# A DFT and a gated FFN on one Trainium2 core: raw weights kept in buffers of `h`, part of the weight fold and of stage 2 moved between FFN steps, and the mirror value matmul behind the next chunk's gate matmuls

## The chip, the cores and the metric

The kernel runs on one core of one Trainium2 chip. The metric is the device time of one execution in microseconds (us); lower is better. Every time quoted is a median of several executions on the chip, with the lowest and highest in brackets. A profile, taken by the hardware profiler, shows one execution of each kernel; its span is about 1.7 us shorter than the time.

The engines are called as the profile calls them: PE is the matmul side of TensorE and PEld its weight loads, DVE is VectorE, ACT is ScalarE, POOL is GpSimd, SP is SyncE (here it only issues DMAs).

## The reference, cut to what matters

```python
# x: (8, 3008, 256) f32; w_gate, w_val: (256, 1536) f32; w_out: (1536, 256) f32
X = np.fft.fft(np.fft.fft(x, axis=1), axis=2).real      # per batch
t = X.reshape(8 * 3008, 256)
out = (np.maximum(t @ w_gate, 0) * (t @ w_val)) @ w_out  # f32
```

The kernel factors the long DFT as 3008 = 94 x 32. The 256-point DFT is not done on the data at all: it is multiplied into the two weight matrices once ("fold of the weights"), which gives three sets of folded weights, `wc` and `ws` for cosine and sine and `wm` = -2·`ws` (with an exception in row 0). The outputs come in pairs of frequencies k and -k. For one chunk of 128 hidden units, "plus" computes the pre-activations of k as `wc·p + ws·q`; "minus" (the mirror) adds `wm·q` into the same PSUM accumulator, which turns it into `wc·p - ws·q`, the pre-activations of -k. `G` and `V` are these accumulators for the gate and the value weights, the tile `pq` holds p and q, `gs` is the rectified G, and `h` is the product of `gs` and V (the gate product).

## The kernel before

There are 8 batches of 3 blocks of 12 chunks: 288 FFN steps. The data of the next batches go through stage 1, a shuffle through DRAM, a rotation and stage 2 in small pieces between the FFN steps. Only batch 0 has to do all that first, together with the tables and the fold of the weights. That is "the start" below.

```python
def fold(b, eng, lo, hi):            # symmetric parts of x; four passes over n rows, on DVE or POOL
    xl, xh, xc, eo = xt[b]
    n = hi - lo
    x1, c1, e1 = xl[:, lo:hi, :], xc[:, lo - 1:hi - 1, :], eo[:, lo:hi, :]
    rev = free(xh[0:NA], (NB // 2 - lo) * D, [-D, n], [1, D])
    eng.tensor_tensor(c1, x1, rev, op=ALU.subtract)
    eng.tensor_tensor(x1, x1, rev, op=ALU.add)
    ...                              # two more passes that write eo, and a small copy

def rotate(b):                       # needs all of the shuffle's loads
    t4 = t4t[b]
    ps = psd.tile([128, 512], F32, tag="d", name="psr")
    nc.tensor.matmul(ps[:, 0:NKA], lhsT=rot[:], rhs=t4[:, :, H], start=True, stop=True)
    nc.vector.tensor_copy(t4[:, :, H], ps[:, 0:NKA])
...
    # ---- the start, in program order (tables left out) ----
    fold(0, nc.vector, 2, 8); fold(0, nc.vector, 8, 12)      # on separate lines in the kernel
    fold(0, nc.gpsimd, 12, 16)
    fold_ends(0, nc.vector)
    fold(0, nc.vector, 1, 2)
    for k, c in enumerate((1, 2, 3, 4, 5, 6, 7, 0)):
        stage1(0, c, "dve" if k in (5, 7) else "act")
    for k in (2, 4, 6, 0):
        shuffle_out(0, k, k + 2)                             # to DRAM
    load_x(1, nc.scalar)                                     # next batch, 1.6 MB and a gather of 1.6 MB
    nc.gpsimd.dma_start(out=wo[:], in_=view(w_out, ...))     # 768 KB
    for blk in range(NBLK):
        shuffle_in(0, 4 * blk, 4 * blk + 4)                  # back from DRAM
    fold_all(1)
    for n in range(DF // 512):                               # fold of the weights, fp32
        for i in range(2):
            for cs in range(2):
                ps = psw.tile([128, 512], F32, tag="w", name="psw")
                for c in range(2):
                    nc.tensor.matmul(ps[:], lhsT=cd[:, c, cs, :], rhs=wst[i][:, c, n * 512:(n + 1) * 512],
                                     start=(c == 0), stop=(c == 1))
                ...                                          # copies to wc, or to ws and wm
    rotate(0)
    for blk in range(NBLK):
        stage2(0, blk, 0, "act"); stage2(0, blk, 1, "dve")
...
def plus(b, blk, f):
    ...                                                      # h, G (psg, 2 buffers), V (psv, 2 buffers)
    for i, acc in enumerate((G, V)):
        nc.tensor.matmul(acc[:], lhsT=wc[i][:, fs], rhs=pq[:, 0, :], start=True, stop=False)
        nc.tensor.matmul(acc[:], lhsT=ws[i][:, fs], rhs=pq[:, 1, :], start=False, stop=True)
    gs = gp.tile([128, 512], F32, tag="gs", name="gs")
    nc.scalar.activation(gs[:], G[:], ACTF.Relu)
    nc.vector.tensor_tensor(h[:, 0, :], gs[:], V[:], op=ALU.mult)      # the gate product

def minus(b, blk, f):
    ...
    for i, acc in enumerate((G, V)):
        nc.tensor.matmul(acc[:], lhsT=wm[i][:, fs], rhs=pq[:, 1, :], start=False, stop=True,
                         skip_group_check=True)
    gs = gp.tile([128, 512], F32, tag="gs", name="gs")
    nc.scalar.activation(gs[:], G[:], ACTF.Relu)
    nc.vector.tensor_tensor(free(h[:], ...), gs[:]..., V[:]..., op=ALU.mult)
...
for b in range(B):
    t0 = b * NBLK * NF
    tl, t1, tr, t2, d2 = (17, 16, 28, 29, 1) if b == 0 else (10, 4, 19, 20, 2)
    ...    # at step t0+tl: load x of b+2; from t0+t1: stage 1 of b+1; t0+tr: rotate; from t0+t2: stage 2
for t in range(n + NF):
    if 0 < t <= n:
        minus(*steps[t - 1])
    if t < n:
        plus(*steps[t])
    for fn in extra.get(t, ()):
        fn()
    if t >= NF:
        out_piece(b, blk, f)           # 8 output matmuls of the step 12 earlier
```

The order of the matmuls in one step is therefore: mirror G, mirror V (of the chunk before), plus G (two), plus V (two), then eight output matmuls. Mirror V overwrites the accumulator that the gate product of the step before reads. The output matmuls lag by 12 steps, so the first 12 steps, called the ramp, have none.

## Time and profile before

The time is 752.1 us (751.9 to 754.2, four executions). Five readings matter.

| reading | value |
|---|---|
| rotation of batch 0 starts | 67.67 us |
| first FFN matmul | 70.87 us |
| first output matmul (ramp 27.55 us long) | 98.42 us |
| median step after that | 2.217 us |
| start of the last output matmul to the end of the span | 5.6 us |

The chain that ended last, from the profile's page, first by engine and then by line:

```profile
PE 82%; DVE 6%; ACT 4%; POOL 3%; issue 3%; DMA 1%; ACTq 0%; POOLq 0%; DVEq 0%
PE po L380 30%; PE V L357 10%; PE G L347 7%; PE G L346 7%; PE V L347 7%; PE V L346 7%; PE G L357 7%; DVE h L350 4%; PE psw L313 3%; ACT gs L360 2%; ACT gs L349 1%; DVE h L362 1%; DMA t_969<-Td 1%; DMA Td<-t_719 1%; DVE q L37 0%
```

Mirror V (L357 V) holds 10% of the chain where each other FFN matmul of the same size holds 7%, and DVE's gate product (L350) holds 4%. Those are the first signs that mirror V is held up by DVE. The table by stages says almost nothing of it. Its columns are the stretch in us, then for PE, PEld, DVE, ACT and POOL the busy time with the number of instructions, then the granted TensorE clock, the DMA share and GB/s:

```profile
60.00:70.00 10.00, 8.69 (x34) 3.90 (x34) 2.98 (x6) 4.03 (x7) 8.67 (x2) 1.00 0.81 154
80.00:90.00 10.00, 7.34 (x29) 2.62 (x28) 6.24 (x10) 5.38 (x9) 9.11 (x7) 1.00 0.14 30
200.00:400.00 200.00, 199.53 (x1331) 126.65 (x1330) 136.96 (x209) 118.74 (x206) 65.93 (x25) 1.00 0.37 94
```

From 200 to 400 us PE is shown busy for 199.53 of 200 us. That looks like a limit with nothing left to gain. It isn't, because the ends of matmuls are modelled: a matmul is drawn 0.38 us long and the next may start 0.215 us after it. The page "Trainium Kernel Development and Optimization" of the Trainium skill (section "Performance Expectations") warns that matmul busy time is a bad measure of how near a kernel is to its limit, since matmuls are pipelined. This trace agrees: PE is drawn busy for 199.53 of 200 us, and only the spacing from start to start shows the hole. Here is one steady step in the timeline (start, duration, engine, line, operation; in brackets, idle time and what ended it):

```profile
277.24 0.69 DVE L350 TENSOR_TENSOR h<-gs,V 128x512 bf16<-128x512 f32 x1
...
277.72 0.38 PE L357 MATMUL G<-pq,wm_91 128*128 128x512 bf16 x1
...
277.99 0.38 PE L357 MATMUL V<-pq,wm_92 128*128 128x512 bf16 x1
...
278.20 0.38 PE L346 MATMUL G<-pq,wc_87 128*128 128x512 bf16 x1
```

The gate product ends at 277.93, and mirror V starts just behind it, at 277.99: 0.27 us after mirror G, where every other pair of these matmuls is 0.215 us apart (277.99 to 278.20). No idle time is drawn at mirror V, because mirror G is still drawn as running. Summed over all steps after 98 us, the spacing from mirror G to mirror V exceeds 215 ns by 14.7 us in total.

In the ramp the same dependence is not hidden in 50 ns but stands alone:

```profile
71.52 0.38 PE L347 MATMUL V<-pq,ws_90 128*128 128x512 bf16 x1
...
71.55 0.60 ACT L349 ACTIVATE gs<-G 128x512 f32<-128x512 f32 x1 [0.23 <-PE G L347]
72.20 0.38 PE L357 MATMUL G<-pq,wm_91 128*128 128x512 bf16 x1 [0.30 <-ACT gs L349]
...
72.23 0.69 DVE L350 TENSOR_TENSOR h<-gs,V 128x512 bf16<-128x512 f32 x1 [0.47 <-ACT gs L349]
...
72.98 0.38 PE L357 MATMUL V<-pq,wm_92 128*128 128x512 bf16 x1 [0.40 <-DVE h L350]
```

A ramp step is a loop of plus G, ACT 0.60, DVE 0.69, mirror V, and takes 2.22 us although its six matmuls take 1.29 us (6 x 0.215).

The third place is the start, again in the timeline:

```profile
20.75 0.30 POOL L35 TENSOR_SCALAR q<-t_204 128x128 f32<-128x128 f32 x1
20.76 1.89 DVE L88 TENSOR_TENSOR xc<-xl,xh 94x1536 f32<-94x1536 f32 x1 [4.67 <-DMA xh<-in_x_dram,ix]
21.14 1.67 POOL L36 TENSOR_SCALAR q<-q 128x128 f32<-128x128 f32 x1
22.69 1.75 DVE L89 TENSOR_TENSOR xl<-xl,xh 94x1536 f32<-94x1536 f32 x1
...
42.06 0.59 PE L117 MATMUL ps_277<-eo,w_82 94*96 94x256 bf16 x2 [8.48 <-POOL eo L92]
...
67.67 0.18 PE L146 MATMUL psr<-t_304,rot 128*128 128x12 bf16 x1 [0.39 <-DMA t_304<-Td]
```

The fold of x ends on POOL at 42.06 us. POOL's 128x128 table operation at 21.14 takes 1.67 us; its neighbour of the same size, started 0.01 us before DVE's fold operation, took 0.30 us. It ends 0.16 us after the DVE operation beside it. The rotation waits for the last load of the shuffle. PE is busy until shortly before it with the fold of the weights, 24 fp32 matmuls of about 0.86 us, which this wait just hides.

### The profile page before, as it was taken

The page shows a single profiled execution, that of the slowest core. Times are in us where ns is not written, and L with a number is a line of the kernel's source. Part 1 is how long each engine was busy: PE and PEld are TensorE (multiplying, and loading weights), DVE is VectorE, ACT ScalarE, POOL GpSimd, SP SyncE. Part 2 cuts the span into 40 slices and gives each one's busy share as a digit, 9 for nine tenths or more (in the row PEclk, how much of TensorE's full clock was granted, in tenths as well). Part 3 has the DMA queues.
Part 4 walks back from the last instruction along what each step waited for, and adds up shares of the span by engine and source line. Part 5 has one row for each costly group of instructions (what it writes and reads, how often), then busy time and mean ns, then how long its engine had stood idle before and what let it go on. Part 6 is the DMA issues. An engine that isn't in the chain of part 4 may idle for free.

```text
span 750.4 us, 12199 instructions
## 1 busy us (share of the span) xinstructions
PE 692.4 (92%) x4432; PEld 430.6 (57%) x4432; DVE 481.0 (64%) x747; ACT 408.3 (54%) x701; POOL 221.6 (30%) x116
## 2 busy tenths in 40 slices
PE   0178799999999999999999999999999999999997
PEld 0033256566666666666666666666666666666565
DVE  6613666666666766766666767666667667666672
ACT  2114556556565656556565655556565655555551
POOL 2837739102920086004900094005800000000000
PEclk9999999999999999999999999999999999999999
DMA  9466253616342534116241454135221141211213
GB/s 195 165 164 113 62 112 93 157 29 151 104 111 57 115 112 113 56 41 172 71 135 33 116 139 111 29 82 143 59 55 29 32 136 28 53 33 28 55 29 82
DMA packets 26971, 67.61 MB, mean 90 GB/s; under 512 B 3856, under 2 KB 17680, under 8 KB 24720
## 3 DMA queue, kind: packets, MB, share of 16 engines
q1 hardware_dynamic: 24340, 51.84, 26.6%
q0 software_dynamic: 2448, 13.37, 8.2%
q10 hardware_dynamic: 124, 1.64, 0.9%
q8 instruction: 34, 0.56, 0.3%
q14 instruction: 25, 0.20, 0.1%
HBM read 36.68 MB, written 30.93 MB: 90 GB/s over the span
## 4 chain that ended last, share of the span: by engine, by line
PE 82%; DVE 6%; ACT 4%; POOL 3%; issue 3%; DMA 1%; ACTq 0%; POOLq 0%; DVEq 0%
PE po L380 30%; PE V L357 10%; PE G L347 7%; PE G L346 7%; PE V L347 7%; PE V L346 7%; PE G L357 7%; DVE h L350 4%; PE psw L313 3%; ACT gs L360 2%; ACT gs L349 1%; DVE h L362 1%; DMA t_969<-Td 1%; DMA Td<-t_719 1%; DVE q L37 0%
## 5 line engine op out<-in xcount | busy, mean ns | idle before, releaser
L362 DVE TENSOR_TENSOR h<-gs,V 128x512 bf16<-128x512 f32 x288 | 198.1, 688 | 203.4 <-ACT gs L360 148.6
L380 PE MATMUL po<-wo,h 128*128 128x256 bf16 x2304 | 296.8, 272 | 0.0
L360 ACT ACTIVATE gs<-G 128x512 f32<-128x512 f32 x288 | 172.2, 598 | 214.1 <-PE G L357 214.1
L380 PEld LDWEIGHTS <-h 128*128 128x128 bf16 x2304 | 222.7, 98 | 64.1 <-issue 2.0
L350 DVE TENSOR_TENSOR h<-gs,V 128x512 bf16<-128x512 f32 x288 | 197.8, 687 | 11.3 <-ACT gs L349 9.9
L349 ACT ACTIVATE gs<-G 128x512 f32<-128x512 f32 x288 | 172.3, 598 | 30.9 <-PE G L347 14.7
L88 POOL TENSOR_TENSOR xc<-xl,xh 94x3840 f32<-94x3840 f32 (+1 forms) x8 | 60.6, 7574 | 302.2 <-DMA xl<-in_x_dram 268.8
L357 PE MATMUL V<-pq,wm_92 128*128 128x512 bf16 x288 | 108.6, 377 | 6.3 <-DVE h L350 4.2
L357 PE MATMUL G<-pq,wm_91 128*128 128x512 bf16 x288 | 109.1, 379 | 3.1 <-ACT gs L349 3.1
L347 PE MATMUL V<-pq,ws_90 128*128 128x512 bf16 x288 | 109.2, 379 | 0.0
L346 PE MATMUL V<-pq,wc_88 128*128 128x512 bf16 x288 | 109.0, 378 | 0.0
L347 PE MATMUL G<-pq,ws_89 128*128 128x512 bf16 x288 | 108.9, 378 | 0.0
L346 PE MATMUL G<-pq,wc_87 128*128 128x512 bf16 x288 | 108.8, 378 | 0.0
L89 POOL TENSOR_TENSOR xl<-xl,xh 94x3840 f32<-94x3840 f32 (+1 forms) x8 | 60.6, 7578 | 0.6
L346 PEld LDWEIGHTS <-wc_87 128*128 128x128 bf16 x288 | 27.7, 96 | 54.5 <-issue 43.2
L347 PEld LDWEIGHTS <-ws_90 128*128 128x128 bf16 x288 | 28.0, 97 | 34.2
L386 ACT COPY os<-po 128x512 f32<-128x512 f32 x48 | 28.1, 586 | 35.6 <-PE po L380 35.6
L346 PEld LDWEIGHTS <-wc_88 128*128 128x128 bf16 x288 | 27.8, 97 | 34.3
L347 PEld LDWEIGHTS <-ws_89 128*128 128x128 bf16 x288 | 27.7, 96 | 34.2
L117 PEld LDWEIGHTS <-w_82 94*96 94x96 bf16 x120 | 15.7, 131 | 50.5 <-issue 28.1
L384 DVE COPY os<-po 128x512 f32<-128x512 f32 x48 | 33.0, 688 | 6.9 <-PE po L380 6.9
L357 PEld LDWEIGHTS <-wm_92 128*128 128x128 bf16 x288 | 28.2, 98 | 9.6 <-issue 6.5
(345 smaller groups left out, 346.8 us busy)
## 6 DMA issues: line engine op xcount, KB each, us to landing
out_dram<-os SPq DMA_DIRECT2D x176, 128.0 KB, 2.1
xl<-in_x_dram SPq DMA_DIRECT2D x7, 1360.0 KB, 9.8
xl<-in_x_dram SPq DMA_DIRECT2D x7, 238.0 KB
wst_103<-in_moe_w_gate_dram SPq DMA_DIRECT2D x2, 768.0 KB, 20.4
wst_106<-in_moe_w_val_dram SPq DMA_DIRECT2D x2, 768.0 KB, 23.7
out_dram<-os SPq DMA_DIRECT2D x16, 96.0 KB, 4.5
xl<-in_x_dram ACTq DMA_DIRECT2D x1, 1360.0 KB
Td<-t_256 SPq DMA_DIRECT2D x4, 192.0 KB, 9.2
```

The costliest lines, as they stand in the source:

```text
L88: eng.tensor_tensor(c1, x1, rev, op=ALU.subtract)
L89: eng.tensor_tensor(x1, x1, rev, op=ALU.add)
L346: nc.tensor.matmul(acc[:], lhsT=wc[i][:, fs], rhs=pq[:, 0, :], start=True, stop=False)
L347: nc.tensor.matmul(acc[:], lhsT=ws[i][:, fs], rhs=pq[:, 1, :], start=False, stop=True)
L349: nc.scalar.activation(gs[:], G[:], ACTF.Relu)
L350: nc.vector.tensor_tensor(h[:, 0, :], gs[:], V[:], op=ALU.mult)
L357: nc.tensor.matmul(acc[:], lhsT=wm[i][:, fs], rhs=pq[:, 1, :], start=False, stop=True, skip_group_check=True)
L360: nc.scalar.activation(gs[:], G[:], ACTF.Relu)
L362: nc.vector.tensor_tensor(free(h[:], 512 + NB - 1, [NB, 16], [-1, NB]), gs[:].rearrange("p (a k) -> p a k", k=NB), V[:].rearrange("p (a k) ...
L380: nc.tensor.matmul(po[:, s % 2, :], lhsT=ht[b, blk, ff][:, sg, g * 128:(g + 1) * 128], rhs=wo[:, ff, :], start=(ff == 0), stop=(ff == NF - 1))
L384: nc.vector.tensor_copy(os_[:, s - 1:s + 1, :], po[:])
L386: nc.scalar.copy(os_[:, s - 1:s + 1, :], po[:])
```

## The change

The intent is to start the FFN steps earlier and to take the hole out of each step. The change has four parts.

1. The raw weights and the DFT table `cd` are now held in tiles of the pool of `h` (which isn't needed before the FFN steps), so that the fold of the weights may run late. It is cut in three: a third between stage-1 parts, a third before the rotation, a third in FFN steps 0 to 3.
2. Stage 2 of blocks 1 and 2 of batch 0 moves to FFN steps 5 to 8, and rotation and stage 2 of batch 1 move one step later.
3. In each step, mirror V moves behind plus G: mirror G, plus G (two), mirror V, plus V (two).
4. At the start, tables of `m2` and `rot` move from POOL to DVE, the table of `cd` moves just before the fold of x, POOL folds six rows instead of four, and stage-1 parts alternate with shuffle stores.

The diff, cut to its core:

```diff
+    hp = ctx.enter_context(tc.tile_pool(name="hp", bufs=2 * NF + 1, space=SB))
+    pso = ctx.enter_context(tc.tile_pool(name="pso", bufs=2, space=PS))
...
+                wst[i, n, c] = hp.tile([128, 512], F32, tag="h", name="wst")
+    cd = [hp.tile([128, 2, H], F32, tag="h", name="cd") for c in range(2)]
...
+    def fold_w(n, i, cs):
+        ps = pso.tile([128, 512], F32, tag="o", name="psw")
+        for c in range(2):
+            nc.tensor.matmul(ps[:], lhsT=cd[c][:, cs, :], rhs=wst[i, n, c][:], start=(c == 0), stop=(c == 1))
+        ...                                     # copies as before
...
-            sin_of(nc, pl, sp, sv[:], t2[:], NB, [128, 4, NB])
+            sin_of(nc, nc.vector, sp, sv[:], t2[:], NB, [128, 4, NB])
...                                             # and the other table operations beside it
-        fold(0, nc.vector, 2, 8)
-        fold(0, nc.vector, 8, 12)
-        fold(0, nc.gpsimd, 12, 16)
+        fold(0, nc.vector, 2, 6)
+        fold(0, nc.gpsimd, 10, 14)
+        fold(0, nc.vector, 6, 10)
+        fold(0, nc.gpsimd, 14, 16)
         fold_ends(0, nc.vector)
         fold(0, nc.vector, 1, 2)
-        for k, c in enumerate((1, 2, 3, 4, 5, 6, 7, 0)):
-            stage1(0, c, "dve" if k in (5, 7) else "act")
-        for k in (2, 4, 6, 0):
-            shuffle_out(0, k, k + 2)
+        for k, (c0, c1) in enumerate(((1, 3), (3, 5), (5, 7), (7, 8), (0, 1))):
+            for c in range(c0, c1):
+                stage1(0, c, "act")
+            shuffle_out(0, c0, c1)
+            if k < 2:
+                for cs in range(2):
+                    fold_w(0, k, cs)
         load_x(1, nc.scalar)
-        nc.gpsimd.dma_start(out=wo[:], in_=view(w_out, ...))
         for blk in range(NBLK):
             shuffle_in(0, 4 * blk, 4 * blk + 4)
+        nc.gpsimd.dma_start(out=wo[:], in_=view(w_out, ...))
         fold_all(1)
-        ...                                     # the whole fold of the weights
+        for i in range(2):
+            for cs in range(2):
+                fold_w(1, i, cs)
     rotate(0)
-    for blk in range(NBLK):
-        stage2(0, blk, 0, "act")
-        stage2(0, blk, 1, "dve")
+    stage2(0, 0, 0, "act")
+    stage2(0, 0, 1, "dve")
...                                             # plus and minus are cut in their G and V halves (i = 0, 1)
+    for k in range(4):
+        at(k, fold_w, 2, k // 2, k % 2)
+        at(5 + k, stage2, 0, 1 + k // 2, k % 2, "dve")
...
-        tl, t1, tr, t2, d2 = (17, 16, 28, 29, 1) if b == 0 else (10, 4, 19, 20, 2)
+        tl, t1, tr, t2, d2 = (17, 16, 29, 30, 1) if b == 0 else (10, 4, 19, 20, 2)
...
-        if 0 < t <= n:
-            minus(*steps[t - 1])
-        if t < n:
-            plus(*steps[t])
+        for i in range(2):
+            if 0 < t <= n:
+                minus(*steps[t - 1], i)
+            if t < n:
+                plus(*steps[t], i)
```

More of the change, by code (lines that the diff above doesn't have):

```diff
@@ L178 @@
     wo = const.tile([128, NF, D], BF16, tag="wo")
-    with tc.tile_pool(name="st", bufs=1, space=SB) as st, \
-         tc.tile_pool(name="sp", bufs=2, space=SB) as sp, \
-         tc.tile_pool(name="psw", bufs=4, space=PS) as psw:
-        wst = []
+    wst = {}
+    for n in range(DF // 512):
         for i, w in enumerate((w_gate, w_val)):
-            t = st.tile([128, 2, DF], F32, tag=f"wst{i}", name=f"wst{i}")
             for c in range(2):
-                nc.sync.dma_start(out=t[:, c, :], in_=w[c * 128:(c + 1) * 128, :])
-            wst.append(t)
+                wst[i, n, c] = hp.tile([128, 512], F32, tag="h", name="wst")
+    cd = [hp.tile([128, 2, H], F32, tag="h", name="cd") for c in range(2)]
+    for n in range(DF // 512):
+        for i, w in enumerate((w_gate, w_val)):
+            for c in range(2):
+                nc.sync.dma_start(out=wst[i, n, c][:], in_=w[c * 128:(c + 1) * 128, n * 512:(n + 1) * 512])
+    def fold_w(n, i, cs):
+        ps = pso.tile([128, 512], F32, tag="o", name="psw")
+        for c in range(2):
+            nc.tensor.matmul(ps[:], lhsT=cd[c][:, cs, :], rhs=wst[i, n, c][:], start=(c == 0), stop=(c == 1))
+        sl_ = slice(n * 512, (n + 1) * 512)
+        if cs == 0:
+            nc.scalar.copy(wc[i][:, sl_], ps[:])
+        else:
+            nc.vector.tensor_copy(ws[i][:, sl_], ps[:])
+            nc.scalar.activation(wm[i][:, sl_], ps[:], ACTF.Copy, scale=s2[:])
+    with tc.tile_pool(name="sp", bufs=2, space=SB) as sp:
         si = sp.tile([NA, J], F32, tag="si")
@@ L212 @@
         nc.vector.memset(w1[:, 0, :], 0.0)
-        cd = st.tile([128, 2, 2, H], F32, tag="cd")
-        for c in range(2):
-            mi = sp.tile([128, 1], F32, tag="mi")
-            nc.gpsimd.iota(mi[:], pattern=[[0, 1]], base=c * 128, channel_multiplier=1,
-                           allow_small_or_imprecise_dtypes=True)
-            dd = sp.tile([128, 2, H], F32, tag="dd")
-            nc.gpsimd.iota(dd[:], pattern=[[0, 2], [1, H]], base=0, channel_multiplier=0,
-                           allow_small_or_imprecise_dtypes=True)
-            nc.vector.memset(dd[:, 1, 0:1], float(H))
-            nc.vector.tensor_scalar(dd[:], dd[:], scalar1=mi[:], scalar2=None, op0=ALU.mult)
-            nc.vector.tensor_scalar(dd[:, 0, :], dd[:, 0, :], scalar1=float(D // 4), scalar2=None, op0=ALU.add)
-            nc.vector.tensor_scalar(dd[:, 1, 0:1], dd[:, 1, 0:1], scalar1=float(D // 4), scalar2=None, op0=ALU.add)
-            sin_of(nc, nc.vector, sp, cd[:, c, :, :], dd[:], D, [128, 2, H])
         pl = nc.gpsimd
@@ L266 @@
                        allow_small_or_imprecise_dtypes=True)
-        pl.tensor_scalar(ui[:], ui[:], scalar1=up[:], scalar2=None, op0=ALU.is_equal)
+        nc.vector.tensor_scalar(ui[:], ui[:], scalar1=up[:], scalar2=None, op0=ALU.is_equal)
         for cs in range(2):
             t2 = sp.tile([128, 4, NB], F32, tag="m2t")
-            pl.tensor_scalar(t2[:], kbi[:], scalar1=mul[:], scalar2=offs[cs][:],
+            nc.vector.tensor_scalar(t2[:], kbi[:], scalar1=mul[:], scalar2=offs[cs][:],
                                     op0=ALU.mult, op1=ALU.add)
             sv = sp.tile([128, 4, NB], F32, tag="m2s")
-            sin_of(nc, pl, sp, sv[:], t2[:], NB, [128, 4, NB])
-            pl.tensor_tensor(m2[:, cs, :].rearrange("p (u k) -> p u k", u=4), sv[:], ui[:], op=ALU.mult)
+            sin_of(nc, nc.vector, sp, sv[:], t2[:], NB, [128, 4, NB])
+            nc.vector.tensor_tensor(m2[:, cs, :].rearrange("p (u k) -> p u k", u=4), sv[:], ui[:], op=ALU.mult)
         di = sp.tile([128, 4, 2, 16], F32, tag="di")
@@ L281 @@
         pl.memset(ro[:], 0.0)
-        pl.tensor_scalar(ro[:, :, 0, 1:16], di[:, :, 0, 1:16], scalar1=16.0, scalar2=-1.0,
+        nc.vector.tensor_scalar(ro[:, :, 0, 1:16], di[:, :, 0, 1:16], scalar1=16.0, scalar2=-1.0,
                                 op0=ALU.is_equal, op1=ALU.mult)
-        pl.tensor_scalar(ro[:, :, 1, 1:16], di[:, :, 1, 1:16], scalar1=-16.0, scalar2=None, op0=ALU.is_equal)
-        pl.tensor_scalar(ro[:, :, :, 0], di[:, :, :, 0], scalar1=0.0, scalar2=None, op0=ALU.is_equal)
-        pl.tensor_copy(rot[:], ro[:].rearrange("p u s j -> p (u s j)"))
+        nc.vector.tensor_scalar(ro[:, :, 1, 1:16], di[:, :, 1, 1:16], scalar1=-16.0, scalar2=None, op0=ALU.is_equal)
+        nc.vector.tensor_scalar(ro[:, :, :, 0], di[:, :, :, 0], scalar1=0.0, scalar2=None, op0=ALU.is_equal)
+        nc.vector.tensor_copy(rot[:], ro[:].rearrange("p u s j -> p (u s j)"))
         pf = sp.tile([128, 1], F32, tag="pf")
@@ L291 @@
         pl.tensor_scalar(s2[:], pf[:], scalar1=1.0, scalar2=-2.0, op0=ALU.min, op1=ALU.mult)
-        fold(0, nc.vector, 2, 8)
-        fold(0, nc.vector, 8, 12)
-        fold(0, nc.gpsimd, 12, 16)
+        for c in range(2):
+            mi = sp.tile([128, 1], F32, tag="mi")
+            nc.gpsimd.iota(mi[:], pattern=[[0, 1]], base=c * 128, channel_multiplier=1,
+                           allow_small_or_imprecise_dtypes=True)
+            dd = sp.tile([128, 2, H], F32, tag="dd")
+            nc.gpsimd.iota(dd[:], pattern=[[0, 2], [1, H]], base=0, channel_multiplier=0,
+                           allow_small_or_imprecise_dtypes=True)
+            nc.vector.memset(dd[:, 1, 0:1], float(H))
+            nc.vector.tensor_scalar(dd[:], dd[:], scalar1=mi[:], scalar2=None, op0=ALU.mult)
+            nc.vector.tensor_scalar(dd[:, 0, :], dd[:, 0, :], scalar1=float(D // 4), scalar2=None, op0=ALU.add)
+            nc.vector.tensor_scalar(dd[:, 1, 0:1], dd[:, 1, 0:1], scalar1=float(D // 4), scalar2=None, op0=ALU.add)
+            sin_of(nc, nc.vector, sp, cd[c][:], dd[:], D, [128, 2, H])
@@ L302 @@
         load_x(1, nc.scalar)
-        nc.gpsimd.dma_start(out=wo[:], in_=view(w_out, 0, [[D, 128], [128 * D, NF], [1, D]]))
         for blk in range(NBLK):
             shuffle_in(0, 4 * blk, 4 * blk + 4)
+        nc.gpsimd.dma_start(out=wo[:], in_=view(w_out, 0, [[D, 128], [128 * D, NF], [1, D]]))
         fold_all(1)
-        for n in range(DF // 512):
-            for i in range(2):
-                for cs in range(2):
-                    ps = psw.tile([128, 512], F32, tag="w", name="psw")
-                    for c in range(2):
-                        nc.tensor.matmul(ps[:], lhsT=cd[:, c, cs, :], rhs=wst[i][:, c, n * 512:(n + 1) * 512],
-                                         start=(c == 0), stop=(c == 1))
-                    sl_ = slice(n * 512, (n + 1) * 512)
-                    if cs == 0:
-                        nc.scalar.copy(wc[i][:, sl_], ps[:])
-                    else:
-                        nc.vector.tensor_copy(ws[i][:, sl_], ps[:])
-                        nc.scalar.activation(wm[i][:, sl_], ps[:], ACTF.Copy, scale=s2[:])
+        for i in range(2):
+            for cs in range(2):
+                fold_w(1, i, cs)
@@ L322 @@
     rotate(0)
-    for blk in range(NBLK):
-        stage2(0, blk, 0, "act")
-        stage2(0, blk, 1, "dve")
+    stage2(0, 0, 0, "act")
+    stage2(0, 0, 1, "dve")
     gp = ctx.enter_context(tc.tile_pool(name="gp", bufs=4, space=SB))
-    hp = ctx.enter_context(tc.tile_pool(name="hp", bufs=2 * NF + 1, space=SB))
     op = ctx.enter_context(tc.tile_pool(name="op", bufs=4, space=SB))
@@ L332, with plus @@
     psv = ctx.enter_context(tc.tile_pool(name="psv", bufs=2, space=PS))
-    pso = ctx.enter_context(tc.tile_pool(name="pso", bufs=2, space=PS))
     steps = [(b, blk, f) for b in range(B) for blk in range(NBLK) for f in range(NF)]
     ht = {}
-    def plus(b, blk, f):
+    def plus(b, blk, f, i):
         pq = pqt[b, blk]
         fs = slice(f * 128, (f + 1) * 128)
-        h = hp.tile([128, 2, 512], BF16, tag="h", name="h")
-        G = psg.tile([128, 512], F32, tag="g", name="G")
-        V = psv.tile([128, 512], F32, tag="v", name="V")
-        ht[b, blk, f] = (h, G, V)
-        for i, acc in enumerate((G, V)):
-            nc.tensor.matmul(acc[:], lhsT=wc[i][:, fs], rhs=pq[:, 0, :], start=True, stop=False)
-            nc.tensor.matmul(acc[:], lhsT=ws[i][:, fs], rhs=pq[:, 1, :], start=False, stop=True)
-        gs = gp.tile([128, 512], F32, tag="gs", name="gs")
-        nc.scalar.activation(gs[:], G[:], ACTF.Relu)
-        nc.vector.tensor_tensor(h[:, 0, :], gs[:], V[:], op=ALU.mult)
@@ L352, in minus @@
-    def minus(b, blk, f):
+        if i == 0:
+            ht[b, blk, f] = {"h": hp.tile([128, 2, 512], BF16, tag="h", name="h"),
+                             0: psg.tile([128, 512], F32, tag="g", name="G"),
+                             1: psv.tile([128, 512], F32, tag="v", name="V")}
+        e = ht[b, blk, f]
+        nc.tensor.matmul(e[i][:], lhsT=wc[i][:, fs], rhs=pq[:, 0, :], start=True, stop=False)
+        nc.tensor.matmul(e[i][:], lhsT=ws[i][:, fs], rhs=pq[:, 1, :], start=False, stop=True)
@@ L353, in minus @@
+        if i == 0:
+            e["gs"] = gp.tile([128, 512], F32, tag="gs", name="gs")
+            nc.scalar.activation(e["gs"][:], e[0][:], ACTF.Relu)
+        else:
+            nc.vector.tensor_tensor(e["h"][:, 0, :], e["gs"][:], e[1][:], op=ALU.mult)
+    def minus(b, blk, f, i):
         pq = pqt[b, blk]
         fs = slice(f * 128, (f + 1) * 128)
-        h, G, V = ht[b, blk, f]
-        for i, acc in enumerate((G, V)):
-            nc.tensor.matmul(acc[:], lhsT=wm[i][:, fs], rhs=pq[:, 1, :], start=False, stop=True,
-                             skip_group_check=True)
@@ L359, in minus @@
-        gs = gp.tile([128, 512], F32, tag="gs", name="gs")
-        nc.scalar.activation(gs[:], G[:], ACTF.Relu)
-        nc.vector.tensor_tensor(free(h[:], 512 + NB - 1, [NB, 16], [-1, NB]),
-                                gs[:].rearrange("p (a k) -> p a k", k=NB),
-                                V[:].rearrange("p (a k) -> p a k", k=NB), op=ALU.mult)
-        ht[b, blk, f] = h
+        e = ht[b, blk, f]
+        nc.tensor.matmul(e[i][:], lhsT=wm[i][:, fs], rhs=pq[:, 1, :], start=False, stop=True,
+                         skip_group_check=True)
@@ L367 @@
+        if i == 0:
+            e["gs"] = gp.tile([128, 512], F32, tag="gs", name="gs")
+            nc.scalar.activation(e["gs"][:], e[0][:], ACTF.Relu)
+        else:
+            nc.vector.tensor_tensor(free(e["h"][:], 512 + NB - 1, [NB, 16], [-1, NB]),
+                                    e["gs"][:].rearrange("p (a k) -> p a k", k=NB),
+                                    e[1][:].rearrange("p (a k) -> p a k", k=NB), op=ALU.mult)
+            ht[b, blk, f] = e["h"]
     state = {}
```

## The prediction

> **What bounds the kernel now.** From about 98 us on, TensorE is the limit: the table by stages shows it 99.7% busy from 100 to 700 us. Start-to-start spacing in the timeline is 215 ns for a 512-column matmul, 109 ns for 256. The one hole in every FFN step: mirror V follows mirror G after 266 ns (median), not 215, because it waits for the DVE gate product (687 ns) of the step before. This hole sums to 14.7 us after 98 us. The first 12 steps have no output matmuls and run at 2.215 us against 1.29 of matmuls (chain G plus -> ACT 0.60 -> DVE 0.69 -> mirror V). At the start the fold of x ends on POOL at 42.1 us, stage 1 at 45.3, then DMA is saturated (5.2 MB from 43 to 67.6 us) and the rotation starts at 67.67 on the last shuffle load; the fp32 weight fold (20.6 us of TensorE) ends at 66.9, just hidden behind it. First FFN matmul 70.87.
>
> **What changes, costed.**
> 1. Order G mirror, G plus, V mirror, V plus: 431 ns of matmuls are put ahead of the wait. The hole nearly vanishes: -13.7 us. In the ramp the loop becomes mirror V -> two DVE products, about 1.85 us a step, but four steps carry a 1.72 us weight fold (about 3.0 us each) and four carry a stage-2 part with a DVE eviction. Ramp: about 28 instead of 25.5 us, +2.4.
> 2. Stage 2 of blocks 1, 2 leaves the start: -1.5 us.
> 3. Rotation of batch 1 one step later: its wait (1.76 us) mostly goes: -1.5 us.
> 4. Start. The weight fold was hidden, so moving it frees nothing; what counts is when x is folded. Table work moves from POOL to DVE ahead of DVE's folds (about 3 us), and POOL folds 6 rows instead of 4, at the same time as DVE. The Trainium skill, "SBUF — State Buffer", section "SBUF: two separate sides", says DVE ops with two SBUF inputs and GpSimd ops exclude each other for a whole instruction. The trace agrees: a 128x128 POOL op of about 0.3 us took 1.67 us beside a DVE fold op and ended 0.16 us after it. So I expect the two to alternate, not to add up: POOL 11.3 + DVE 10.3 + remaining tables about 4.5 us from about 18 us, ending near 43 to 45. The ws copies stand behind all folds on DVE, and ACT's wm and later stage-1 evictions behind ws, so the last shuffle store is issued near 50 us (was 45.3). The DMA volume after the second gather starts is the same, so rotation near 67 to 71: +1 us.
>
> Sum: 752.1 - 13.7 + 2.4 - 1.5 - 1.5 + 1 = about **739 us**, 8 in 10 between 731 and 745. Faster by over 2%: 0.36; within 2%: 0.62; slower by over 2%: 0.02.
>
> **What the profile would show.** (1) mirror matmul of V no longer idle before it, DVE h gone from the chain of waits; steady steps 2.16 us instead of 2.21. (2) Ramp: first four steps 3.0, later 1.85 to 2.1 us. (3) POOL and DVE fold ops of batch 0 stretched to about the sum of both. (4) ACT waiting for DVE ws before stage-1 evictions; rotation released by the shuffle load at 67 to 71 us.
>
> **What would make it wrong.** If DVE and POOL folds really overlap, x is folded by about 35 us and rotation comes 5 to 7 us earlier: near 732. If the shuffle store queues behind the next x load: near 745.

## The result, and the profile after

The changed kernel takes 739.35 us (738.33 to 739.39, four executions), against 752.13 us (751.88 to 754.24) for the kernel before, measured in the same rounds. The ratio is 0.982, with a 95% interval of 0.980 to 0.984. Ratios here are the mean time of one kernel's runs over that of the other's of the same rounds, so not quite the ratio of the medians quoted. Executions over 1.5% slower than the fastest of the same kernel are left out of the means. The difference is real, and inside the 2% that the verdict calls "same".

The chain of the kernel after:

```profile
PE 88%; DVE 4%; DMA 4%; issue 1%; ACT 1%; POOL 1%; SPq 0%; POOLq 0%
PE po L392 34%; PE G L355 9%; PE V L367 9%; PE V L354 8%; PE G L367 8%; PE V L355 8%; PE G L354 7%; PE psw L199 2%; DMA Td<-t_280 2%; DVE q L37 1%; DMA t_986<-Td 1%; DVE h L360 1%; DMA Td<-t_736 1%; DMA t_346<-Td 1%; DVE q L36 0%
```

PE's share rose from 82 to 88%, and the gate product (now L360) fell from 4 to 1%. The six FFN matmuls now hold about equal shares. The table by stages:

```profile
60.00:70.00 10.00, 0.04 (x2) 0.07 (x3) 0.00 (x0) 0.00 (x0) 5.11 (x1) 0.66 0.78 144
70.00:80.00 10.00, 9.59 (x34) 4.68 (x36) 3.57 (x6) 3.81 (x7) 9.92 (x2) 0.82 0.01 2
200.00:400.00 200.00, 198.68 (x1330) 129.34 (x1353) 133.47 (x213) 112.77 (x209) 65.81 (x25) 1.00 0.36 93
```

PE does almost nothing from 60 to 70 us, and its granted clock falls to 0.66 there and is still 0.82 in the next stretch (asked more finely, it is 0.50 from 63.3 to 73.5 us and 1.00 before and behind). Below, "cold" means this halved clock and "warm" the full one. From 200 to 400 us, PE's drawn busy time is *less* than before (198.68 against 199.53), and that is because some matmul records are missing from this trace (the page counts 4353 matmuls, and 4432 weight loads). The weight loads, 1353 in this stretch against 1330, show the faster steps. Drawn busy time is no measure here, for this reason too.

One steady step after:

```profile
277.02 0.68 DVE L360 TENSOR_TENSOR h<-gs,V 128x512 bf16<-128x512 f32 x1
...
277.45 0.38 PE L367 MATMUL G<-pq,wm_97 128*128 128x512 bf16 x1
...
277.67 0.38 PE L354 MATMUL G<-pq,wc_93 128*128 128x512 bf16 x1
...
278.10 0.38 PE L367 MATMUL V<-pq,wm_98 128*128 128x512 bf16 x1
```

The gate product ends at 277.70, and mirror V is not due until 278.10. The matmuls follow each other every 0.215 us and the median step is 2.169 us. To 0.01 us that is the sum of its matmuls: 6 x 0.215 and 8 x 0.109.

The start after, in the timeline:

```profile
18.80 2.34 POOL L91 TENSOR_TENSOR xc<-xl,xh 94x1024 f32<-94x1024 f32 x1 [1.38 <-DMA xh<-in_x_dram,ix]
18.92 2.37 DVE L37 TENSOR_TENSOR q<-t_206,q 128x128 f32<-128x128 f32 x1
...
21.66 2.04 DVE L277 TENSOR_TENSOR m_90<-sv,ui 128x128 bf16<-128x128 f32 x1 [0.38 <-ACT sv L38]
...
44.57 0.69 ACT L205 ACTIVATE wm_97<-psw,s_92 128x512 bf16<-128x512 f32 x1 [2.81 <-DVE ws_95 L204]
...
45.15 0.57 ACT L129 CAST t_280<-ps_299 96x512 bf16<-96x512 f32 x1
...
69.97 0.18 PE L149 MATMUL psr<-t_346,rot 128*128 128x12 bf16 x1 [11.92 <-DMA t_346<-Td]
...
71.10 0.69 DVE L165 CAST pq<-ps_388 128x512 bf16<-128x512 f32 x1 [0.70 <-PE ps_388 L160]
71.25 0.59 PE L354 MATMUL G<-pq,wc_93 128*128 128x512 bf16 x1 [0.19 <-ACT pq L163]
...
71.84 0.59 PE L355 MATMUL G<-pq,ws_95 128*128 128x512 bf16 x1
...
72.65 0.63 PE L355 MATMUL V<-pq,ws_96 128*128 128x512 bf16 x1 [0.22 <-issue]
...
73.08 0.81 PE L199 MATMUL psw<-wst,cd 128*128 128x512 f32 x1
```

Now it is DVE's small table operations that take 2.37 and 2.04 us beside POOL's fold. ACT waits for DVE's `ws` copy, and stage 1's copies (L129) wait behind ACT. The rotation has PE idle before it, and the matmuls behind it run cold: the one at 72.65 is followed after 0.43 us instead of 0.215 (the one at 71.84 had to wait for DVE's copy of `pq` as well, which ends at 71.79, so the 0.59 us before it are not the clock alone).

Where the 12.8 us between the two spans (750.4 and 737.6) lie, read from the starts of the named matmuls:

| stretch | before, us | after, us | difference |
|---|---|---|---|
| start of the span to the rotation | 67.67 | 69.97 | +2.3 |
| rotation to first plus G | 3.20 | 1.29 | -1.9 |
| first plus G to first output matmul (ramp) | 27.55 | 29.66 | +2.1 |
| first output matmul to last mirror G | 635.53 | 620.27 | -15.3 |
| last mirror G to the end | 16.43 | 16.38 | -0.05 |

The fourth line holds the hole between mirror G and mirror V (14.7 us of excess over 0.215 us before; after, where two plus G stand between them, 0.7 us over 3 x 0.215; -14.0) and the wait for the rotation of batch 1 (1.76 us before, 0.31 after, -1.45).

### The profile page after: what moved, and what is told of

It reads as the page before. It is cut to its first block, busy times and chain, and to the rows that moved or that the text cites. A ratio compares the mean times of both kernels' runs of the same rounds, so it can differ in the third digit from the quotient of the medians.

```text
span 737.6 us, 12137 instructions
## 1 busy us (share of the span) xinstructions
PE 674.2 (91%) x4353; PEld 431.6 (59%) x4432; DVE 470.9 (64%) x762; ACT 380.9 (52%) x701; POOL 213.4 (29%) x106
## 4 chain that ended last, share of the span: by engine, by line
PE 88%; DVE 4%; DMA 4%; issue 1%; ACT 1%; POOL 1%; SPq 0%; POOLq 0%
PE po L392 34%; PE G L355 9%; PE V L367 9%; PE V L354 8%; PE G L367 8%; PE V L355 8%; PE G L354 7%; PE psw L199 2%; DMA Td<-t_280 2%; DVE q L37 1%; DMA t_986<-Td 1%; DVE h L360 1%; DMA Td<-t_736 1%; DMA t_346<-Td 1%; DVE q L36 0%
## 5 line engine op out<-in xcount | busy, mean ns | idle before, releaser
L360 DVE TENSOR_TENSOR h<-gs,V 128x512 bf16<-128x512 f32 x288 | 195.9, 680 | 1.6 <-PE V L355 1.6
L91 POOL TENSOR_TENSOR xc<-xl,xh 94x3840 f32<-94x3840 f32 (+2 forms) x9 | 61.8, 6872 | 296.3 <-DMA xl<-in_x_dram 277.7
L367 PE MATMUL V<-pq,wm_98 128*128 128x512 bf16 x288 | 109.1, 379 | 2.0 <-DVE h L360 1.1
L367 PE MATMUL G<-pq,wm_97 128*128 128x512 bf16 x288 | 109.1, 379 | 1.2 <-ACT gs L358 1.2
L355 PE MATMUL G<-pq,ws_95 128*128 128x512 bf16 x283 | 107.5, 380 | 2.8
L354 PE MATMUL V<-pq,wc_94 128*128 128x512 bf16 x287 | 108.8, 379 | 0.0
L355 PE MATMUL V<-pq,ws_96 128*128 128x512 bf16 x267 | 101.4, 380 | 0.2 <-issue 0.2
L354 PE MATMUL G<-pq,wc_93 128*128 128x512 bf16 x236 | 89.6, 380 | 0.2 <-ACT pq L163 0.2
L92 POOL TENSOR_TENSOR xl<-xl,xh 94x3840 f32<-94x3840 f32 (+2 forms) x9 | 61.9, 6875 | 0.7
L354 PEld LDWEIGHTS <-wc_94 128*128 128x128 bf16 x288 | 28.2, 98 | 37.3 <-issue 4.4
L355 PEld LDWEIGHTS <-ws_96 128*128 128x128 bf16 x288 | 28.2, 98 | 34.2 <-issue 0.3
L355 PEld LDWEIGHTS <-ws_95 128*128 128x128 bf16 x288 | 28.2, 98 | 34.2 <-issue 0.4
L367 PEld LDWEIGHTS <-wm_98 128*128 128x128 bf16 x288 | 28.2, 98 | 33.9
## 6 DMA issues: line engine op xcount, KB each, us to landing
xl<-in_x_dram ACTq DMA_DIRECT2D x1, 1360.0 KB, 11.4
```

Of the source, the lines that this page charges most:

```text
L354: nc.tensor.matmul(e[i][:], lhsT=wc[i][:, fs], rhs=pq[:, 0, :], start=True, stop=False)
L355: nc.tensor.matmul(e[i][:], lhsT=ws[i][:, fs], rhs=pq[:, 1, :], start=False, stop=True)
L360: nc.vector.tensor_tensor(e["h"][:, 0, :], e["gs"][:], e[1][:], op=ALU.mult)
L367: nc.tensor.matmul(e[i][:], lhsT=wm[i][:, fs], rhs=pq[:, 1, :], start=False, stop=True, skip_group_check=True)
```

## The experiments

Nine kernels ran, all in three rounds and all correct. The kernel before had medians of 752.3, 752.1 and 752.0 us in the three sets of rounds, which ran on three chips. The kernel after did not run in these sets, so differences from its 739.35 us are taken across sets.

### Only the new order of a step

The first question is whether the order alone explains the gain, and what the rest of the change is worth. This kernel is the one before with `plus` and `minus` cut in halves, and only this in the loop:

```diff
-        if 0 < t <= n:
-            minus(*steps[t - 1])
-        if t < n:
-            plus(*steps[t])
+        for i in range(2):
+            if 0 < t <= n:
+                minus(*steps[t - 1], i)
+            if t < n:
+                plus(*steps[t], i)
```

> The kernel before with nothing changed but the order of the FFN step (G mirror, G plus, V mirror, V plus). Theory: the steady hole of 14.7 us between mirror G and mirror V closes to under 1 us, and the first 12 steps go from 2.21 to about 1.85 us (a loop over the two DVE products) because no weight fold stands in them: 752.1 - 14.0 - 4.4 = about 734, five us better than the whole change. Rival: the order only pays together with the moved start (the weight fold and stage 2 that fill the ramp), and alone it gives clearly less than the whole change, 742 or more.

Measured: 735.24 us (733.60 to 735.76), ratio 0.977 [0.975, 0.979]. The kept trace is of the fastest execution (733.60 us). In it the excess from mirror G to mirror V falls to 0.7 us, as in the kernel after, and the ramp from 27.55 to 22.79 us, with steps of 1.82 us. The change of order alone beats the whole change by about 4 us. The rest of the change, taken together, costs time.

### All but the new order

The counterpart is the kernel after, with the old order of the loop (mirror G, mirror V, plus G, plus V):

```diff
-        for i in range(2):
-            if 0 < t <= n:
-                minus(*steps[t - 1], i)
-            if t < n:
-                plus(*steps[t], i)
+        if 0 < t <= n:
+            for i in range(2):
+                minus(*steps[t - 1], i)
+        if t < n:
+            for i in range(2):
+                plus(*steps[t], i)
```

> The changed kernel with the old order of the FFN step back, all else kept. Theory: the hole of 14.0 us comes back, and the eight ramp steps without a weight fold go from 1.8 to 2.2 us (+3.3): 739.4 + 14.0 + 3.3 = about 757, so the rest of the change costs some 4 us by itself. Rival: the moves at the start are worth something by themselves, and this is at or under the kernel before, 752.

Measured: 763.83 us (762.95 to 764.53), ratio 1.015 [1.013, 1.017]. The sign was right and the size was wrong by 7 us. The excess after mirror G is back at 14.2 us behind the first output matmul, as expected. But two steps near the rotation of batch 1 take 7.92 and 3.72 us, and that rotation starts at 149.24 on its shuffle load. The gather of x for batch 3 had been issued at 136.2 us, before this load, which was issued at 139.1.

### The first third of the weight fold behind stage 1

The two theories were that the start is held by the volume of transfers that stand before the shuffle loads (A), or by the wait of stage-1 copies for `ws` (B). So the part of the weight fold that stands between stage-1 parts moves behind them:

```diff
-            if k < 2:
-                for cs in range(2):
-                    fold_w(0, k, cs)
...
-        for i in range(2):
-            for cs in range(2):
-                fold_w(1, i, cs)
+        for m in range(2):
+            for i in range(2):
+                for cs in range(2):
+                    fold_w(m, i, cs)
```

> The changed kernel with the first third of the weight fold behind all of stage 1 instead of between its parts. The evictions of stage 1 no longer stand behind the ws copy, so the last shuffle store and the load of batch 1 are issued near 44 us instead of 50.7. Theory A (DMA volume from the second gather on sets the rotation): rotation within 1.5 us of 69.97 and time 739 +- 1.5. Theory B (the last shuffle store sets it): rotation near 63 and time near 733.

Measured: 743.65 us, but the four executions are 738.69, 748.83, 738.25 and 748.62 us, so the kernel has two times, 10 us apart. The trace (of a long execution) settles the question of the start: stage 1 ends 6 us earlier (its last copy starts about 44.5 us instead of 50.6), and the rotation only 1.5 us earlier, at 68.46 instead of 69.97. That is theory A. The wait of stage 1 cost about 1.5 us.

The two times come from elsewhere. In the long execution, these are the gather of x for batch 3 (POOL), the issue of the shuffle load of batch 1 (SPq) and the rotation that needs it:

```profile
133.87 0.95 POOL L79 DMA_INDIRECT xh<-in_x_dram,ix  x1
...
134.97 0.38 SPq L143 DMA_DIRECT2D t<-Td  x1
...
146.48 0.18 PE L149 MATMUL psr<-t,rot 128*128 128x12 bf16 x1 [6.67 <-DMA t<-Td]
```

And the same three in the kernel after, where the rotation isn't held up:

```profile
134.91 0.38 SPq L143 DMA_DIRECT2D t_986<-Td  x1
...
137.08 0.94 POOL L79 DMA_INDIRECT xh<-in_x_dram,ix  x1
...
139.97 0.18 PE L149 MATMUL psr<-t_986,rot 128*128 128x12 bf16 x1
```

In the long execution the DMA records show only the 16 KB pieces of the gather from 135 to 141 us, and the 512-byte pieces of the shuffle load almost all from 142 us on, though the load was issued only 1.1 us after the gather. It landed 11.5 us after its issue, where the same load took 5.0 us in the kernel after. The Trainium skill ("DMA: Bandwidth & Descriptors", section "Queues, rings and completion order") says that a DMA engine drains a whole packet, of about 9 to 17 descriptors, from one queue before it turns to the next. The gather's 96 rows over 16 engines are 6 each, so one such packet could hold them all. The trace fits that, though its records don't name the engine: no 512-byte piece started before 141.1 us, and the gather's pieces ran from 135.5 to 143.4 us. In the kernel after, the order is the other way round by 2.2 us. The kernel before had less, 0.6 us (load at 132.32, gather at 132.89), and its load was not held up either (landed after 5.3 us). In the two traces with the gather issued first, by 1.1 us here and by 2.8 us in the experiment before, the load was late. No run measured more finely how much lead either needs.

### All folds of batch 0 on DVE

The prediction held that DVE and POOL exclude each other in the fold. If so, POOL's six rows cost DVE more than doing them itself would. POOL's two folds go to DVE:

```diff
         fold(0, nc.vector, 2, 6)
-        fold(0, nc.gpsimd, 10, 14)
         fold(0, nc.vector, 6, 10)
-        fold(0, nc.gpsimd, 14, 16)
+        fold(0, nc.vector, 10, 14)
+        fold(0, nc.vector, 14, 16)
```

> The changed kernel with all of batch 0's fold on DVE: POOL folds nothing, DVE six rows more (about 6.1 us of its own work). Theory (DVE and POOL ops exclude each other, and POOL takes 2.3 ns an element against 1.04): DVE's table work is no longer held up from 18.8 to 31 us, the fold ends near 40 us instead of 42.5 although DVE does more, rotation near 67.7, time near 737. Rival (they overlapped and POOL's share was a help): the fold ends near 48 us, rotation near 75, time near 745.

Measured: 737.02 us (736.57 to 737.83), ratio 0.980 [0.978, 0.981], 2.3 us below the kernel after. The same table operations on DVE, now with POOL out of the way, and the end of the fold:

```profile
18.88 0.29 DVE L37 TENSOR_TENSOR q<-t,q 128x128 f32<-128x128 f32 x1
...
24.00 1.22 DVE L91 TENSOR_TENSOR xc<-xl,xh 94x1024 f32<-94x1024 f32 x1
...
39.57 0.16 DVE L95 CAST eo<-xl 94x2 bf16<-94x2 f32 x1
```

The operation that took 2.37 us takes 0.29. DVE's folds begin at 24.0 instead of 32.8 us and end at 39.7 instead of 42.5, though DVE does six rows more. The rotation comes at 66.92 instead of 69.97. So POOL's help was worth less than nothing. The Trainium skill says as much ("SBUF — State Buffer", section "SBUF: two separate sides"): a DVE operation with two SBUF inputs and a GpSimd operation that reads SBUF take the shared port pair for a whole instruction each. The trace agrees in both directions: 0.30 became 1.67 us on POOL before, 0.29 became 2.37 us on DVE after.

### The new order, with the rotation of batch 1 one step later

With the new order alone, the rotation of batch 1 waits about 2.2 us, since the steps before it became faster. This kernel is the first experiment with that part of the change added:

```diff
-        tl, t1, tr, t2, d2 = (17, 16, 28, 29, 1) if b == 0 else (10, 4, 19, 20, 2)
+        tl, t1, tr, t2, d2 = (17, 16, 29, 30, 1) if b == 0 else (10, 4, 19, 20, 2)
```

> The kernel before with the new order and the rotation and stage 2 of batch 1 one step later (as the change has them). In the run with the order alone the rotation of batch 1 held TensorE for 2.2 us. Theory: that wait goes, and 735.2 becomes about 733.1; nothing else moves. If it stays at 735 the wait has only moved.

Measured: 732.25 us (731.78 to 732.35), ratio 0.971 with a wide interval [0.963, 0.980]. Two of the seven runs of the kernel before in this set were disturbed. The one of 1892.63 us counts as slow and is left out; the one of 761.98 us stays in and widens the interval. The median before, 752.12, is as in the other sets. In the traces the step before the rotation is down from 4.30 to 2.17 us, as expected. The medians differ by 3.0 us (735.24 and 732.25), 0.9 more than that. The granted clock was 0.995 to 0.999 in the executions of the first experiment and 0.999 to 1.000 here; the two traces, at 0.999 and 1.000, have spans 1.8 us apart. So the rest seems to come from the clock in the first experiment's executions and not from the rotation; no run tests that.

### The next loads behind the shuffle

If the volume of transfers before the shuffle loads holds the rotation (theory A above), then holding back what nobody needs yet, the load of batch 1 and of `w_out`, should bring the rotation far forward. A one-element copy on POOL from the shuffled tile makes the gather wait for the shuffle without any new semaphore:

```diff
-        load_x(1, nc.scalar)
         for blk in range(NBLK):
             shuffle_in(0, 4 * blk, 4 * blk + 4)
+        seen = const.tile([1, 1], BF16, tag="seen", name="seen")
+        nc.gpsimd.tensor_copy(seen[:], t4t[0][0:1, NKA - 1, 0:1])
+        load_x(1, nc.sync)
...
-        tl, t1, tr, t2, d2 = (17, 16, 29, 30, 1) if b == 0 else (10, 4, 19, 20, 2)
+        tl, t1, tr, t2, d2 = (17, 18, 31, 32, 1) if b == 0 else (10, 4, 19, 20, 2)
```

> The changed kernel with the loads of batch 1 and of w_out issued behind the shuffle loads of batch 0 instead of ahead of them (a one-element POOL copy that reads the shuffled tile holds POOL's queue back; stage 1, rotation and stage 2 of batch 1 two steps later so that they don't wait). Theory (the volume ahead of the shuffle sets the start): 3.9 MB less ahead of it, rotation near 58.5 us instead of 69.97, set by the last shuffle store issued at 50.7; TensorE stays warm; time near 727. Rival (the shuffle's own small packets are what takes the time): rotation stays above 66 and the time above 735.

Measured: 727.12 us (726.64 to 728.41), ratio 0.964 [0.956, 0.973] (same set, with the 761.98 us run). The issue of the shuffle loads and the rotation, first in the kernel after, then here:

```profile
65.04 1.48 SPq L143 DMA_DIRECT2D t_346<-Td  x3
...
69.97 0.18 PE L149 MATMUL psr<-t_346,rot 128*128 128x12 bf16 x1 [11.92 <-DMA t_346<-Td]
```

```profile
52.45 1.48 SPq L143 DMA_DIRECT2D t<-Td  x3
...
58.58 0.18 PE L149 MATMUL psr<-t,rot 128*128 128x12 bf16 x1 [1.71 <-DMA t<-Td]
```

The rotation starts 11.4 us earlier than in the kernel after, and 1.5 us of it are given back where stage 1 of batch 1 waits for POOL's fold of its x. So the start was bound by the order of transfers. The change moved only the load of `w_out` behind the shuffle loads in the program; POOL's queue, which waits for nothing there, issued it at 43.41 us all the same (43.23 before).

### The parts that paid, together

This kernel takes the new order, all folds on DVE as soon as x has landed, the table of `cd` before and those of `m2` and `rot` after the fold, no weight fold within stage 1, half of it before the rotation and half in steps 0 to 5, stage 2 of blocks 1 and 2 in steps 7 to 10, and the next loads behind the shuffle. Its core, against the kernel after:

```diff
+        ...                                    # table of cd moved up, m2 and rot moved behind stage 1
         fold(0, nc.vector, 2, 6)
-        fold(0, nc.gpsimd, 10, 14)
         fold(0, nc.vector, 6, 10)
-        fold(0, nc.gpsimd, 14, 16)
+        fold(0, nc.vector, 10, 14)
+        fold(0, nc.vector, 14, 16)
...
-            if k < 2:
-                for cs in range(2):
-                    fold_w(0, k, cs)
...                                             # seen and load_x(1) behind the shuffle, batch 1 two steps later, as above
-        for i in range(2):
+        for n, i in ((0, 0), (0, 1), (1, 0)):
             for cs in range(2):
-                fold_w(1, i, cs)
+                fold_w(n, i, cs)
...
+    for k in range(6):
+        at(k, fold_w, 1 + (k > 1), (k // 2 + 1) % 2, k % 2)
     for k in range(4):
-        at(k, fold_w, 2, k // 2, k % 2)
-        at(5 + k, stage2, 0, 1 + k // 2, k % 2, "dve")
+        at(7 + k, stage2, 0, 1 + k // 2, k % 2, "dve")
```

> What the experiments so far point to, together: new order; fold of batch 0 on DVE alone, starting when x lands (cosine table before it, stage-2 tables and rotation matrix after it); no weight fold between the parts of stage 1, half of it in the wait for the shuffle and half in ramp steps 0 to 5; stage 2 of blocks 1, 2 in steps 7 to 10; loads of batch 1 and of w_out behind the shuffle. Theory: fold ends near 35 us, last shuffle store near 37, rotation near 46, ramp near 31 us instead of 29.7, no hole later: 739.4 - 24 + 1.5 = about 717, range 711 to 724. If the start is limited by something else (TensorE in the ramp, or batch 1 arriving late), 725 to 735.

Measured: 718.74 us (718.44 to 719.50), ratio 0.954 [0.945, 0.962] (same set again). It is 33 us faster than the kernel before and 20.6 us faster than the kernel after. In its timeline:

```profile
37.48 0.38 SPq L143 DMA_DIRECT2D t<-Td  x1
...
46.95 0.59 PE L199 MATMUL psw<-wst,cd 128*128 128x512 f32 x1
47.38 0.18 PE L149 MATMUL psr<-t,rot 128*128 128x12 bf16 x1
...
49.52 0.38 PE L353 MATMUL G<-pq,wc 128*128 128x512 bf16 x1 [0.68 <-ACT pq L163]
```

The first shuffle load is issued at 37.5 us, and the rotation follows PE's own weight fold instead of a DMA. Here it should pay to put half of the weight fold into the steps, since the wait that used to hide it is gone: a piece takes 1.72 us of PE before the rotation and lengthens a ramp step by 1.2 us (3.01 less 1.82). That is an estimate from these traces; no run had this kernel with another split. Nor was each of its parts taken out singly. The first FFN matmuls run at full clock (starts 0.215 us apart).

### Two tests of the race

If the 10 us between the two times of the weight-fold experiment, and the miss of the old-order experiment, come from the gather of batch 3 being issued before the shuffle load of batch 1, then stage 1 of batch 1 two steps earlier makes the shuffle load come first every time. Both get the same edit:

```diff
-        tl, t1, tr, t2, d2 = (17, 16, 29, 30, 1) if b == 0 else (10, 4, 19, 20, 2)
+        tl, t1, tr, t2, d2 = (17, 14, 29, 30, 1) if b == 0 else (10, 4, 19, 20, 2)
```

> The run with the weight fold behind stage 1 had two times, 738.5 and 748.7 us; in its profile the shuffle load of batch 1 was issued 1.1 us after the gather of batch 3 and landed behind all of it, and TensorE waited 6.8 us for the rotation. Here stage 1 of batch 1 runs two steps (4.3 us) earlier, its rotation where it was. Theory (the order of those two transfers decides): the shuffle load is always ahead, and every run is at 738 to 739.5. Rival (something else, such as the chip's state, makes the slow times): some runs near 748 again.

Measured, weight fold behind stage 1: 737.65 us (737.19 to 738.59); all four executions are of the short kind. The rotation of batch 1 starts at 139.08 us instead of 146.48.

> The changed kernel with the old order, which came out at 763.8 instead of the expected 757, with stage 1 of batch 1 two steps earlier. Theory: the miss of 7 us is the rotation of batch 1 waiting behind the gather of batch 3; with the shuffle load ahead of the gather the time is 756.5 +- 1.5. Rival: the old order costs more than the hole and the ramp, and it stays above 761.

Measured, old order: 755.54 us (755.03 to 755.97), ratio 1.004 [1.002, 1.006], 8.3 us below the old-order kernel without the edit. So the miss was the race, and all of the change but the order, with stage 1 of batch 1 two steps earlier, costs 3.6 us against the kernel before (755.54 to 751.95 in this set).

## Why the prediction was right, point by point

The predicted 739.0 us met 739.35. The terms of the order, of stage 2 and of the rotation hold one by one. The start cost 1.3 us more than expected, and the other terms together about 1 us less, so that the sum came within 0.4 us is in part luck. So is the size of the ramp term, which holds a cost that the prediction had not put in (the clock, below).

- **The hole, -13.7 us.** Measured -14.0. The trace shows the mechanism, and the first two experiments isolate it: the order alone takes the excess to 0.7 us, as in the kernel after, and the rest without the order leaves it at 14.2.
- **Ramp, +2.4 us.** Measured +2.1. The first steps take 3.01, 3.01, 3.01 and 2.64 us, later ones mostly 1.82. The order alone shortened the ramp by 4.8 us (27.55 to 22.79). The moved weight fold and stage 2 turned that into a loss: four pieces of 1.72 us of fp32 matmuls now stand where PE has only about 0.5 us of slack per step (1.82 less 1.29).
- **Stage 2 out of the start, -1.5 us.** Measured -1.9.
- **Rotation of batch 1, -1.5 us.** Measured -1.45. The fifth experiment isolates it: added to the new order, where the wait was longer, the same move takes 2.1 us off the step (4.30 to 2.17).
- **The start, +1 us.** Measured +2.3. The mechanism was right: POOL and DVE alternated, though not in the operations that the prediction named. It expected the folds of both to be stretched; POOL's folds (18.8 to 30.6 us) stretched DVE's table operations, and DVE's folds, which came from 32.8 us on, took 1.22 us for 94x1024 as in the fourth experiment without POOL. The fold ended at 42.5 us (43 to 45 expected), the last shuffle store went out at about 50.7 us (50 expected), and the rotation came in the expected range of 67 to 71 us. The volume of transfers then absorbed most of the delay, as the third and sixth experiments show.

Two things that matter were not in the prediction, and the sum did not fail for lack of them because they are small. The first is the clock. Because the weight fold moved, PE idles 11.9 us before the rotation, the granted clock drops, and the stretch from the first plus G to the first mirror G takes 3.76 us instead of 2.57 in the combined kernel, which does the same matmuls warm. Of these 1.2 us, about 0.4 are the wait for DVE's copy of `pq` (0.59 less 0.215), and about 0.8 are left for the clock. The sixth experiment confirms the split: it does the same matmuls warm with the same wait for `pq` (0.58 us), and this stretch takes 2.94 us, its whole ramp 28.85 instead of 29.66. The 0.8 us lie inside the ramp's +2.1. Without them the ramp would have cost +1.3 against +2.4 forecast: its fourth step (2.64 us, 3.0 forecast) and the steps with stage 2 (mostly 1.82 us, up to 2.1 forecast) were cheaper than expected. That these errors nearly cancel is luck. The second is that the 2.2 us margin between the shuffle load and the gather of batch 3 was not looked at. It held in the kernel after (and 0.6 us held in the kernel before), and the order of the two was reversed in two of the experiments, with costs of 8 to 10 us. The prediction did not say either that the order alone would beat the whole change, though its numbers imply it: a ramp step of 1.85 us from the order, set against four steps of 3.0 us from the moved weight fold.

What stays open: the trace of the weight-fold experiment is of a long execution, so the order of the two issues in its short ones is inferred from the kernel with stage 1 two steps earlier; why long and short alternate was not studied. The effect of the weights arriving in 2 KB pieces instead of 6 KB (x was complete at 18.8 us instead of 20.8) was seen, not isolated.

## What to carry to other kernels

Look at the spacing of matmul starts, not at busy time: a dependence that costs 50 ns a step is invisible at 99.7% busy and was worth 14 us here. Before moving work out of the start, ask what hides it where it stands: the weight fold was free behind a DMA wait, and moving it into the steps cost TensorE time there, left TensorE to run cold, and didn't move the wait, which fell only when unneeded transfers were put behind needed ones. When a schedule shifts the issue of large gathers, check which small, urgent transfer is issued just beside them.

## What the Trainium skill lacked or had wrong

- "TensorE: Matmul & The Clock Gate", section "Back-to-back issue gap", gives about 131 ns per matmul as the sustained rate at 512 columns in a stream of weight loads and matmuls, and about 216 ns for the isolated gap. Here the stream itself runs at 215 ns for 512 columns and 109 ns for 256, over hundreds of steps with a weight load for each matmul; 131 ns was never seen.
- The same page, Part 1 ("The HAM clock gate"), says that the clock halves after an idle window of about 3.4 us. This agrees (PE was idle for 11.9 us, and the granted clock was 0.50 from 63.3 us, within this wait, to 73.5 us), and a cold 512-column matmul was followed after 0.43 us, as the page's formula for the cold gap has it (427 ns). Nothing is to be mended there; what the page lacks is the reverse case, a kernel that turns cold because work was moved *out* of a wait.
- "DMA: Bandwidth & Descriptors", section "Queues, rings and completion order", states the arbitration but not what follows for a schedule: in two traces a gather of 96 rows of 16 KB went through nearly whole ahead of a load issued 1.1 or 2.8 us later, which landed after 11.5 and 10.1 us instead of 5.0. One kernel took 738 or 749 us, and only 737 to 739 us once the load was issued first.
- "SBUF — State Buffer", section "SBUF: two separate sides", says that one engine blocks the other, but no page found gives a figure for the cost of sharing an elementwise job between DVE and GpSimd: here DVE's own table operations grew from 0.29 to 2.37 us, the fold ended at 42.5 instead of 39.7 us, and the whole kernel lost 2.3 us against DVE alone (739.35 and 737.02).
